# Retention and early-exit experts on one core: two tokens per partition row, 64x64 tiles of TensorE, and scatters without an order

## The chip, the core and the metric

The kernel runs on one core of one Trainium2 chip. The metric is the device time of one execution in microseconds (us). Times inside an execution come from the hardware profiler. TensorE (PE) multiplies, PEld is its loading of weights, VectorE is DVE, ScalarE is ACT, GpSimd is POOL, and SyncE (SP) issues transfers.

## What is computed

The reference has two stages. The first is a retention recurrence over 4 batches, 8 heads, 768 tokens and 64 dimensions per head, in fp32; the second lets a part of the 3072 token rows through one of 8 experts.

```python
for t in range(S):
    state = gamma * state + outer(k[t], v[t])      # per batch and head
    y[t] = scale * q[t] @ state
x = y as rows (token, 512)
do_compute = x @ w_skip > 0                        # other rows: out = x
e_idx, gate_w = top 1 of softmax(xc @ w_gate)
out[row] = x[row] + gate_w * (relu(x[row] @ w1[e_idx]) @ w2[e_idx])
```

## The kernel before

**Retention** runs in 16 units; a unit is one batch and two heads, whose two times 64 dimensions fill 128 partitions. Each unit is cut into 6 chunks of 128 tokens. `load` (L68) brings q and k of a unit so that each partition holds 6 successive tokens of a head (runs of 1536 B), and v with the token of a chunk as partition (runs of 256 B), all on SP's queue; q and k have two buffers each, v four. `scale_qk` (L173) multiplies q and k on POOL with powers of gamma, into `qks`. `t_qk` (L184) transposes them on TensorE, three 128x128 blocks into one PSUM bank with the tag T (two buffers), and ScalarE copies each bank to `QT` or `KT`, writing every sixth element, which puts the tokens back in order (L192, L193). `t_kn` (L195) transposes five chunks of `KT` back, into `Kn` with tokens as partitions. `s_at` (L206) makes the scores of a chunk for each head, 64 rows of contraction and 128 columns of keys, three chunks a call, and VectorE multiplies them with the triangular mask into `ATm` (L216). `s_kv` (L222) makes the state of each chunk from `Kn` and v (128 rows, 64 columns, 64 moving), and VectorE adds the states up into `Zb` (L230 to L238). `s_inter` (L240) adds what earlier chunks contribute and `s_av` (L253) the chunk's own values (128 rows, 64 columns, 128 moving) into one PSUM bank for each half of the chunks, `Y`; ScalarE copies it to `xT` (L263). `t_x` (L265) transposes `xT` to rows, VectorE copies them to `xall`, and SP stores a batch in six transfers.

An fp32 matmul shows as two instructions in the profile, a transpose as one.

**Gate.** Per batch, `gate_logits` (L283) and `gate_rows` (L295) find the expert, the weight and the slot of each row, and `slot_table` (L358) gathers row numbers into a table of 256 slots for each expert. They use a PSUM bank of their own, tag G.

**Experts.** The weights of the first four experts are loaded during retention by POOL's queue (fp32 in memory, bf16 on the chip); those of the last four go out after the retention stage's buffers are free (L495 to L497). `gather` (L443) fetches 128 rows of an expert by index, `x_tr` (L452) casts and transposes them, `layer1` (L462) and `layer2` (L476) multiply; for each half of 128 slots VectorE writes the new rows to `yo` (L485, four buffers), and POOL issues an indirect scatter of them to `out` (L488). `out` is one tensor, so that each scatter waits for the one before it to land.

**Order.** The loop at L379 writes out the order of one turn by hand: the transposes of unit i, the state part and the values of unit i-1, then scores, output transposes and states. From it a scheduler works out the order on each engine, allots buffers, and sets the waits; it moves work forward where the engine would be idle by its own reckoning.

Of the kernel before, what the change touches and what calls it, by code (L numbers as in the profile page):

```python
# [18 lines left out]
def kernel(  # L19
# [15 lines left out]

    nc = tc.nc
# [8 lines left out]
    R = S // 128  # L45
# [22 lines left out]
    def load(i):  # L68
        if i >= NU:
            return  # L70
        b, p = divmod(i, NP)
        hs = slice(2 * p, 2 * p + 2)
        qw[i] = pool.tile([128, 2, R * D], FP32, tag="qw", bufs=2, name="qw")
        kw[i] = pool.tile([128, 2, R * D], FP32, tag="kw", bufs=2, name="kw")
        vn[i] = pool.tile([128, 2, NCH, D], FP32, tag="vn", bufs=4, name="vn")
        nc.sync.dma_start(out=qw[i][:, :, :], in_=q[b, hs].rearrange("h (p r) d -> p h (r d)", p=128))
        nc.sync.dma_start(out=kw[i][:, :, :], in_=k[b, hs].rearrange("h (p r) d -> p h (r d)", p=128))
        for h in range(2):
# [6 lines left out]

    nrow_i = poolC.tile([128, R], I32, name="nrow_i")
    G_.iota(nrow_i[:, :], pattern=[[1, R]], base=0, channel_multiplier=R)
    nrow = poolC.tile([128, R], FP32, name="nrow")
    V_.tensor_copy(nrow[:, :], nrow_i[:, :])
    nlg = poolC.tile([128, H, R], FP32, name="nlg")  # L90
    for h in range(H):
        V_.tensor_scalar(nlg[:, h, :], nrow[:, :], lng[h], None, ALU.mult)
    tq = poolC.tile([128, H, R], FP32, name="tq")
    tk = poolC.tile([128, H, R], FP32, name="tk")
# [9 lines left out]
    maskc = poolC.tile([128, 128], FP32, name="maskc")  # L104
    make_upper_triangular(nc, maskc[:, :], val=1.0, diag=True)
# [27 lines left out]
    G_.iota(chv_i[:, :], pattern=[[1, NCHT]], base=0, channel_multiplier=0)  # L133
    row_i = poolC.tile([128, NCHT], I32, name="row_i")
    G_.iota(row_i[:, :], pattern=[[0, NCHT]], base=1, channel_multiplier=1)
# [32 lines left out]
    QT, KT, Kn, AT, ATm, KV, Y, xT, xall = {}, {}, {}, {}, {}, {}, {}, {}, {}  # L168
# [4 lines left out]
    def scale_qk(i):  # L173
        if i >= NU:
            return
        p = i % NP
        hs = slice(2 * p, 2 * p + 2)
        for w, t in ((qw, tq), (kw, tk)):
            o = pool.tile([128, R, 2, D], FP32, tag="qks", bufs=4, name="qks")
            sc = t[:, hs, :].rearrange("p h r -> p r h").unsqueeze(3).to_broadcast([128, R, 2, D])  # L180
            G_.tensor_tensor(o[:, :, :, :], w[i][:, :, :].rearrange("p h (r d) -> p r h d", d=D), sc, ALU.mult)  # L181
            w[i] = o

    def t_qk(i, w, dst, tag, bufs, a):  # L184

        if a == 0:
            dst[i] = pool.tile([128, S], FP32, tag=tag, bufs=bufs, name=tag)
        ps = ptile()
        for r in range(HB):
            in_ = w[i][:, a * HB + r, :, :].rearrange("p h d -> p (h d)")  # L190
            PE.transpose(out=ps[:, r * 128 : (r + 1) * 128], in_=in_, identity=ident[:, :])  # L191
        o = dst[i][:, :].rearrange("p (t r) -> p r t", r=R)[:, a * HB : (a + 1) * HB, :]  # L192
        A_.copy(out=o, in_=ps[:, :].rearrange("p (r t) -> p r t", r=HB))  # L193

    def t_kn(i, a):  # L195

        n = HB if a == 0 else HB - 1
        if a == 0:
            Kn[i] = pool.tile([128, NCH - 1, 128], FP32, tag="Kn", bufs=2, name="Kn")
        ps = ptile()  # L200
        for r in range(n):
            c = a * HB + r
# [37 lines left out]
    def s_inter(i, a):  # L240
        Y[i, a] = psum.tile([128, HW], FP32, tag=f"Y{a}", bufs=1, name="yps")
        first = True
        for r in range(HB):
            c = a * HB + r
            if c == 0:
                continue
# [318 lines left out]
```

## Time and profile before

| | us |
|---|---|
| median of 3 runs | 321.63 |
| lowest and highest of them | 320.69 and 322.49 |
| the profiled execution, its own time | 322.3 |
| span in it, first to last instruction | 320.4 |
| TensorE matmul busy | 240.1 (75%) |
| TensorE weight load busy | 183.8 (57%) |
| VectorE busy | 132.5 (41%) |
| ScalarE busy | 102.5 (32%) |
| GpSimd busy | 96.0 (30%) |

The mean granted clock of TensorE is 0.882 of full speed. Busy times are sums over stages with different limits; which engine bounds a stage is read from views of that stage. Neighbouring matmuls overlap in the records, so the time of a group is taken from its start to the start of the next group.

### The profile page before, as it was taken

What the parts mean: (1) busy time and instruction counts of PE and PEld (TensorE: products, weight loads), DVE (VectorE), ACT (ScalarE), POOL (GpSimd) and SP (SyncE); (2) the same over time, 40 slices, a digit from 0 to 9 for tenths busy, and PEclk for the clock granted to TensorE, in tenths of its full rate; (3) what the DMA queues carried; (4) which work ended last, traced back from release to release, by engine and by line L of the source; (5) the groups of instructions that cost most, each with busy time, mean ns of one, the idle gap of its engine ahead of it and who ended that gap; (6) DMA issues with size and microseconds to landing.
All of it is one profiled execution on the core that took longest, in us unless ns stands there. A gap on an engine that the chain in (4) does not pass through costs nothing. (4 is left out here: it accounts for less than half of the span.)

```text
span 320.4 us, 5739 instructions
## 1 busy us (share of the span) xinstructions
PE 240.1 (75%) x2253; PEld 183.8 (57%) x2253; DVE 132.5 (41%) x456; ACT 102.5 (32%) x175; POOL 96.0 (30%) x96
## 2 busy tenths in 40 slices
PE   1897999966999998999999993087995009889200
PEld 1676887746887687878787752065764004556000
DVE  4145444634666538854379436032423003223100
ACT  2462466421544454444743420021333000222000
POOL 7325550305331133213300001778500003222321
PEclk9998999995799999999999995569999557999855
DMA  8999999999994872353300023977999971111110
GB/s 215 229 198 250 248 217 213 233 209 295 336 237 102 271 213 70 91 149 101 147 3 0 2 84 114 233 250 182 175 210 209 210 141 49 42 66 54 52 74 28
DMA packets 53438, 49.67 MB, mean 155 GB/s; under 512 B 28074, under 2 KB 44458, under 8 KB 53408
## 3 DMA queue, kind: packets, MB, share of 16 engines
q0 software_dynamic: 15104, 24.07, 36.9%
q1 hardware_dynamic: 38304, 25.19, 28.3%
q8 instruction: 20, 0.33, 0.4%
q14 instruction: 10, 0.08, 0.1%
HBM read 56.64 MB, written 10.49 MB: 210 GB/s over the span
## 5 line engine op out<-in xcount | busy, mean ns | idle before, releaser
L216 DVE TENSOR_TENSOR ATm<-atps,maskc 128x384 f32<-128x384 f32 x64 | 32.7, 553 | 67.3 <-PE atps L214 67.3
L480 PE MATMUL yps<-w2b,hT 128*128 128x512 bf16 x128 | 31.3, 396 | 22.0 <-DVE yo L485 22.0
L191 PE MATMUL tps<-ident,qks 128*128 128x128 f32 x192 | 39.7, 304 | 10.7 <-POOL qks L181 6.5
L193 ACT COPY QT<-tps 128x384 f32<-128x384 f32 x32 | 26.0, 863 | 66.6 <-PE tps L191 66.6
L473 ACT ACTIVATE hT<-hps 128x512 bf16<-128x512 f32 x32 | 19.0, 597 | 82.3 <-PE hps L469 63.0
L181 POOL TENSOR_TENSOR qks<-qw,tq 128x768 f32<-128x768 f32 x16 | 23.9, 1495 | 61.1 <-PE tps L191 41.1
L214 PE MATMUL atps<-QT,KT 64*128 64x128 f32 x384 | 38.5, 298 | 0.0
L488 POOL DMA_INDIRECT out_dram<-yo,si x16 | 15.7, 980 | 71.7 <-DVE yo L485 38.9
L191 PEld LDWEIGHTS tps<-ident,qks 128*128 128x128 f32 x192 | 25.1, 156 | 20.3 <-POOL qks L181 8.0
L181 POOL TENSOR_TENSOR qks<-kw,tk 128x768 f32<-128x768 f32 x16 | 24.0, 1498 | 39.4 <-DMA kw<-in_k_dram 29.3
L214 PEld LDWEIGHTS atps<-QT,KT 64*128 64x128 f32 x384 | 32.3, 194 | 5.7 <-issue 2.8
L485 DVE SCALAR_TENSOR_TENSOR yo<-yps,g,xg 128x512 f32<-128x512 f32 x16 | 12.0, 750 | 53.8 <-DMA out_dram<-yo,si 48.7
L480 PEld LDWEIGHTS <-hT 128*128 128x128 bf16 x128 | 12.7, 101 | 36.6 <-issue 24.8
L469 PE MATMUL hps<-xgT,w1b 128*128 128x256 bf16 x256 | 31.5, 281 | 1.7 <-ACT hT L473 1.7
L247 PE MATMUL yps<-QT,Zb 128*128 128x128 f32 x160 | 30.4, 297 | 0.0
L238 DVE TENSOR_TENSOR Zb<-kvps,Zb 64x64 f32<-64x64 f32 x128 | 28.5, 222 | 4.0
L469 PEld LDWEIGHTS <-w1b 128*128 128x128 bf16 x256 | 25.8, 101 | 7.5 <-issue 2.0
L193 ACT COPY KT<-tps 128x384 f32<-128x384 f32 x32 | 25.6, 864 | 8.9 <-PE tps L191 8.8
L257 PE MATMUL yps<-ATm,vn 128*64 128x128 f32 x384 | 26.9, 280 | 0.0
L247 PEld LDWEIGHTS yps<-QT,Zb 128*128 128x128 f32 x160 | 25.7, 209 | 1.4 <-DVE Zb L236 0.7
L257 PEld LDWEIGHTS yps<-ATm,vn 128*64 128x64 f32 x384 | 21.6, 138 | 2.8 <-issue 1.3
L263 ACT COPY xT<-yps 128x384 f32<-128x384 f32 x32 | 15.3, 489 | 14.6 <-PE yps L257 14.2
(101 smaller groups left out, 248.3 us busy)
## 6 DMA issues: line engine op xcount, KB each, us to landing
w1b<-in_moe_w_dram POOLq DMA_DIRECT2D x8, 1024.0 KB
w2b<-in_moe_w_dram POOLq DMA_DIRECT2D x8, 1024.0 KB
qw<-in_q_dram SPq DMA_DIRECT2D x16, 384.0 KB, 5.4
kw<-in_k_dram SPq DMA_DIRECT2D x16, 384.0 KB, 5.1
vn<-in_v_dram SPq DMA_DIRECT2D x32, 192.0 KB, 4.8
out_dram<-xall SPq DMA_DIRECT2D x24, 256.0 KB, 3.1
xg<-out_dram,gi POOLq DMA_INDIRECT x16
out_dram<-yo,si POOLq DMA_INDIRECT x16
```

The costliest lines, as they stand in the source:

```text
L181: G_.tensor_tensor(o[:, :, :, :], w[i][:, :, :].rearrange("p h (r d) -> p r h d", d=D), sc, ALU.mult)
L191: PE.transpose(out=ps[:, r * 128 : (r + 1) * 128], in_=in_, identity=ident[:, :])
L193: A_.copy(out=o, in_=ps[:, :].rearrange("p (r t) -> p r t", r=HB))
L214: PE.matmul(out=ps[h][:, r * C : (r + 1) * C], lhsT=KT[i][hp, cs], rhs=QT[i][hp, cs], start=True, stop=True)
L216: V_.tensor_tensor(out=ATm[i][:, h, a * HB : (a + 1) * HB, :], in0=ps[h][:, :].rearrange("p (c t) -> p c t", c=HB), in1=maskc[:, :].unsque ...
L238: V_.tensor_tensor(z, kv, Zb[i % 2][c - 1][hp, hp], ALU.add)
L247: PE.matmul(out=Y[i, a][:, r * C : (r + 1) * C], lhsT=Zb[i % 2][c - 1][:, :], rhs=QT[i][:, c * C : (c + 1) * C], start=first, stop=False, ...
L257: PE.matmul(out=Y[i, a][64 * h : 64 * h + 64, r * C : (r + 1) * C], lhsT=vn[i][:, h, c, :], rhs=ATm[i][:, h, c, :], start=False, stop=True ...
L469: PE.matmul(out=ps[:, f, :], lhsT=w1b[e][:, db, fb * 128 : (fb + 1) * 128], rhs=xgT[e][:, db, :], start=(db == 0), stop=(db == NDB - 1),)
L473: A_.activation(out=hT[:, 2 * f2 : 2 * f2 + 2, :], in_=ps[:, :, :], func=AF.Relu, bias=0.0, scale=1.0)
L480: PE.matmul(out=ps[:, :], lhsT=hT[:, fb, st * 128 : (st + 1) * 128], rhs=w2b[e][:, fb, :], start=(fb == 0), stop=(fb == NFB - 1),)
L488: G_.indirect_dma_start(out=out[:, :], out_offset=bass.IndirectOffsetOnAxis(ap=si[:, st, e : e + 1], axis=0), in_=yo[:, :], in_offset=None ...
```

## The change

q, k and v are all loaded with two successive tokens in each partition row (runs of 512 B), three groups of 256 tokens a head; one transfer for v instead of two. A chunk of 128 tokens is then half of the partitions of a group, with its even and its odd tokens in two slots. Transposed blocks go to `QT` and `KT` without a stride, and the k that POOL scaled serves the states directly, so `t_kn` and `Kn` go. Scores, states and values are cut into 64x64 tiles: two heads by two chunks, each with 64 rows of contraction and 64 columns, the row halves writing to different PSUM banks. States take two banks, so the gate's bank is given up and the gate uses the two of tag T. The mask becomes 16 pieces of 64x64. The copies of `t_x` move from VectorE to ScalarE; a batch is stored in three transfers after its second half. The turn is put in another order, and output transposes and gate come one unit later. In the expert stage the scatters of the first pass are declared free of dependence on each other. Row numbers in the table, and scale factors, follow the new layout.

```diff
-    R = S // 128
+    R = 2
+    G = S // (128 * R)
...
+        for w, src, tag, bufs in ((kw, k, "kw", 2), (qw, q, "qw", 2), (vn, v, "vn", 4)):
+            w[i] = pool.tile([128, 2 * G, R * D], FP32, tag=tag, bufs=bufs, name=tag)
             nc.sync.dma_start(
-                out=vn[i][:, h, :, :], in_=v[b, 2 * p + h].rearrange("(c p) d -> p c d", p=128)
+                out=w[i][:, :, :],
+                in_=src[b, hs].rearrange("h s d -> (h s) d").rearrange("(g p r) d -> p g (r d)", p=128, r=R),
             )
...
+    maskc = poolC.tile([128, 4, R, 64], FP32, name="maskc")
+    for r in range(4):
+        for rq in range(R):
+            for hi in range(2):
+                V_.memset(maskc[64 * hi : 64 * hi + 64, r, rq, :], 1.0)
+                G_.affine_select(
+                    out=maskc[64 * hi : 64 * hi + 64, r, rq, :], in_=maskc[64 * hi : 64 * hi + 64, r, rq, :],
+                    pattern=[[R, 64]], base=rq - r % 2, channel_multiplier=-R, compare_op=ALU.is_ge, fill=0.0,
+                )
...
+        for w, t, tag in ((kw, tk, "ks"), (qw, tq, "qs")):
+            o = pool.tile([128, NCH, 2, D], FP32, tag=tag, bufs=2, name=tag)
+            sc = t[:, hs, :].rearrange("p h c -> p c h").unsqueeze(3).to_broadcast([128, NCH, 2, D])
+            in_ = w[i][:, :, :].rearrange("p (h g) (r d) -> p (g r) h d", h=2, d=D)
+            G_.tensor_tensor(o[:, :, :, :], in_, sc, ALU.mult)
...
-    def t_kn(i, a):
-
...
+        for j in range(HB):
+            in_ = w[i][:, a * HB + j, :, :].rearrange("p h d -> p (h d)")
+            PE.transpose(out=ps[:, j * 128 : (j + 1) * 128], in_=in_, identity=ident[:, :])
+        A_.copy(out=dst[i][:, a * HB : (a + 1) * HB, :], in_=ps[:, :].rearrange("p (j t) -> p j t", j=HB))
...
+        for j in range(HB):
+            s_ = a * HB + j
+            g = s_ // R
+            for c in range(2):
+                for h in range(2):
+                    hp = slice(64 * h, 64 * h + 64)
+                    cp = slice(64 * c, 64 * c + 64)
+                    PE.matmul(
+                        out=ps[h][cp, j * C : (j + 1) * C], lhsT=KT[i][hp, s_, cp], rhs=QT[i][hp, R * g : R * g + R, cp],
+                        start=True, stop=True,
+                    )
...
+                in1=maskc[:, a : a + HB, :, :].rearrange("p c r t -> p c (r t)"), op=ALU.mult,
...
+        ps = [psum.tile([128, G * D], FP32, tag=f"KV{c}", bufs=1, name="kvps") for c in range(2)]
+        for g in range(G):
+            for r in range(R):
+                for c in range(2):
+                    if 2 * g + c == NCH - 1:
+                        continue
+                    cp = slice(64 * c, 64 * c + 64)
+                    for h in range(2):
+                        PE.matmul(
+                            out=ps[c][64 * h : 64 * h + 64, g * D : (g + 1) * D], lhsT=kw[i][cp, R * g + r, h, :],
+                            rhs=vn[i][cp, h * G + g, r * D : (r + 1) * D], start=(r == 0), stop=(r == R - 1),
+                        )
...
+    def s_inter(i):
+        for c in range(2):
+            Y[i, c] = psum.tile([128, G, C], FP32, tag=f"Y{c}", bufs=1, name="yps")
+        for ch in range(1, NCH):
+            g, c = divmod(ch, 2)
...
+    def s_av(i):
+        for g in range(G):
+            for r in range(R):
+                for c in range(2):
+                    cp = slice(64 * c, 64 * c + 64)
+                    for h in range(2):
+                        PE.matmul(
+                            out=Y[i, c][64 * h : 64 * h + 64, g, :], lhsT=vn[i][cp, h * G + g, r * D : (r + 1) * D],
+                            rhs=ATm[i][cp, h, R * g + r, :], start=False, stop=(r == R - 1), skip_group_check=True,
+                        )
+        xT[i] = pool.tile([128, NCH, 128], FP32, tag="xT", bufs=6, name="xT")
+        for c in range(2):
+            A_.copy(
+                out=xT[i][:, :, 64 * c : 64 * c + 64], in_=Y[i, c][:, :, :].rearrange("p g (r t) -> p (g r) t", r=R)
+            )
...
+        for j in range(HB):
+            PE.transpose(out=ps[:, j * 128 : (j + 1) * 128], in_=xT[i][:, a * HB + j, :], identity=ident[:, :])
+        A_.copy(
+            out=xall[b][:, a * HB : (a + 1) * HB, p * 128 : (p + 1) * 128],
+            in_=ps[:, :].rearrange("p (j t) -> p j t", j=HB),
...
+        if p == NP - 1 and a == 1:
+            for g in range(G):
+                row0 = b * S + g * 128 * R
+                nc.sync.dma_start(
+                    out=out[row0 : row0 + 128 * R, :].rearrange("(p r) d -> p r d", r=R),
+                    in_=xall[b][:, R * g : R * g + R, :],
+                )
...
+            gp = ptile("gps")
...
-    for i in range(NU + 3):
+    for i in range(NU + 5):
         if i < NU:
+            scale_qk(i + 1)
             load(i + 3)
-            scale_qk(i + 1)
-            t_qk(i, qw, QT, "QT", 3, 0)
-            t_qk(i, qw, QT, "QT", 3, 1)
+            t_qk(i, kw, KT, "KT", 2, 0)
+            t_qk(i, qw, QT, "QT", 2, 0)
+            t_qk(i, kw, KT, "KT", 2, 1)
+            t_qk(i, qw, QT, "QT", 2, 1)
+        if 2 <= i < NU + 2:
+            t_x(i - 2, 0)
         if 1 <= i <= NU:
-            s_inter(i - 1, 0)
-            s_inter(i - 1, 1)
+            s_inter(i - 1)
+        if 2 <= i < NU + 2:
+            t_x(i - 2, 1)
         if i < NU:
-            t_qk(i, kw, KT, "KT", 2, 0)
-            t_qk(i, kw, KT, "KT", 2, 1)
+            s_at(i, 0)
+            s_kv(i)
         if 1 <= i <= NU:
-            s_av(i - 1, 0)
-            s_av(i - 1, 1)
+            s_av(i - 1)
         if i < NU:
-            t_kn(i, 0)
-            t_kn(i, 1)
-            s_at(i, 0)
             s_at(i, 1)
-        if 1 <= i <= NU:
-            t_x(i - 1, 0)
-            t_x(i - 1, 1)
-        if i < NU:
-            s_kv(i)
-        if i >= 1:
-            b, p = divmod(i - 1, NP)
+        if i >= 2:
+            b, p = divmod(i - 2, NP)
             if p == NP - 1 and b < B:
                 gs[b] = gate_logits(b)
             if p == 0 and b >= 1:
                 gate_rows(b - 1, gs[b - 1])
             if p == 1 and b >= 1:
-                slot_table(pool, psum, list(range((b - 1) * NCH, b * NCH)), "G")
+                slot_table(pool, psum, list(range((b - 1) * NCH, b * NCH)), "T", 2)
...
-            G_.indirect_dma_start(
+            sc = G_.indirect_dma_start(
                 out=out[:, :], out_offset=bass.IndirectOffsetOnAxis(ap=si[:, st, e : e + 1], axis=0),
                 in_=yo[:, :], in_offset=None, bounds_check=N - 1, oob_is_err=False,
             )
+            if first:
+                for o in scatters:
+                    tc.declare_no_dep(sc.ins, o.ins, reason="the slots of a pass name distinct rows")
+                scatters.append(sc)
```

## Rows read from the trace of the kernel before

**Rows 1.** Windows by stage: us, busy (instructions) per engine, PEclk, DMA share, GB/s.

```profile
0.00:78.30 78.30, 62.51 (x595) 50.59 (x596) 33.72 (x127) 31.23 (x51) 31.20 (x38) 0.93 1.10 229
78.30:188.00 109.70, 105.60 (x1158) 86.33 (x1160) 67.59 (x241) 50.17 (x88) 25.48 (x18) 0.97 0.45 131
...
244.70:263.50 18.80, 0.17 (x4) 0.05 (x1) 0.01 (x1) 0.60 (x1) 0.00 (x0) 0.59 1.04 190
263.50:298.50 35.00, 31.67 (x193) 18.73 (x192) 10.01 (x17) 7.16 (x12) 9.78 (x10) 0.93 0.13 53
```

**Rows 2.** The chain that ended last, its shares of the span by line.

```profile
by line: DMA out_dram<-yo,si 6.9%; issue 2.8%; POOL out_dram L488 0.3%; POOLq L488 0.1%; POOLq L520 0.0%
```

**Rows 3.** Waits: who waited for whom, us in total, times, longest.

```profile
DVE yo L485 <- DMA out_dram<-yo,si: 48.7, 12, 20.6
...
PE yps L480 <- DVE yo L485: 22.0, 4, 19.4
```

**Rows 4.** Timeline of POOL, VectorE and TensorE around the scatters: start, us, what.

```profile
226.13 0.98 POOL L165 DMA_DIRECT2D w2b<-in_moe_w_dram  x1
227.42 1.06 POOL L488 DMA_INDIRECT out_dram<-yo,si  x1 [0.30 <-DVE xb L456]
...
263.49 0.75 DVE L485 SCALAR_TENSOR_TENSOR yo<-yps,g,xg 128x512 f32<-128x512 f32 x1 [20.55 <-DMA out_dram<-yo,si]
264.25 1.05 POOL L488 DMA_INDIRECT out_dram<-yo,si  x1 [35.60 <-DVE yo L485]
...
294.88 3.62 PE L480 MATMUL yps<-w2b,hT 128*128 128x512 bf16 x16
...
313.74 0.97 POOL L488 DMA_INDIRECT out_dram<-yo,si  x1 [2.48 <-DMA out_dram<-yo,si]
```

**Rows 5.** Timeline of TensorE: sixth, seventh and last retention unit.

```profile
74.41 1.33 PE L226 MATMUL kvps<-vn,Kn 128*64 128x64 f32 x18 [4.91 <-DMA vn<-in_v_dram]
...
78.26 1.52 PE L191 MATMUL tps<-ident,qks 128*128 128x128 f32 x6
...
174.12 0.86 PE L191 MATMUL tps<-ident,qks 128*128 128x128 f32 x6
```

**Rows 6.** Timeline of TensorE over one plain unit, 141.37 to 150.92.

```profile
141.37 0.80 PE L226 MATMUL kvps<-vn,Kn 128*64 128x64 f32 x20
142.10 0.55 PE L191 MATMUL tps<-ident,qks 128*128 128x128 f32 x3
...
145.60 1.53 PE L257 MATMUL yps<-ATm,vn 128*64 128x128 f32 x24
147.06 0.77 PE L203 MATMUL tps<-ident,KT 128*128 128x128 f32 x5
147.75 0.94 PE L214 MATMUL atps<-QT,KT 64*128 64x128 f32 x12
148.62 0.76 PE L272 MATMUL tps<-ident,xT 128*128 128x128 f32 x5
149.33 1.40 PE L214 MATMUL atps<-QT,KT 64*128 64x128 f32 x12
150.66 0.33 PE L272 MATMUL tps<-ident,xT 128*128 128x128 f32 x1
150.92 0.80 PE L226 MATMUL kvps<-vn,Kn 128*64 128x64 f32 x20
```

**Rows 7.** ScalarE's copies, by lines: busy us, mean ns.

```profile
L193 ACT COPY KT<-tps 128x384 f32<-128x384 f32 x32 | 25.6, 864 | 8.9 <-PE tps L191 8.8
...
L263 ACT COPY xT<-yps 128x384 f32<-128x384 f32 x32 | 15.3, 489 | 14.6 <-PE yps L257 14.2
```

**Rows 8.** Timeline of TensorE: the shortest spacing of small matmuls.

```profile
173.81 0.47 PE L368 MATMUL tabps<-rhsT,oh 128*128 128x40 bf16 x12
```

**Rows 9.** Windows with q alone, then the end of k with v.

```profile
104.20:105.60 1.40, 1.40 (x26) 1.23 (x21) 0.00 (x0) 1.30 (x4) 1.39 (x1) 1.00 0.48 126
106.80:108.50 1.70, 1.70 (x18) 1.40 (x15) 1.48 (x3) 0.00 (x0) 0.00 (x0) 1.00 0.90 281
```

**Rows 10.** POOL's selection of the mask, by lines.

```profile
masks.py:66 POOL TENSOR_SCALAR_AFFINE_SELECT maskc<-maskc 128x128 f32<-128x128 f32 x1 | 0.3, 285 | 0.0
```

More of the change, by code (lines that the diff above doesn't have):

```diff
@@ L209, in s_at @@
         ps = [psum.tile([128, HW], FP32, tag=f"AT{h}", bufs=1, name="atps") for h in range(2)]
-        for r in range(HB):
-            cs = slice((a * HB + r) * C, (a * HB + r + 1) * C)
-            for h in range(2):
-                hp = slice(64 * h, 64 * h + 64)
-                PE.matmul(out=ps[h][:, r * C : (r + 1) * C], lhsT=KT[i][hp, cs], rhs=QT[i][hp, cs], start=True, stop=True)
+        for j in range(HB):
[9 more added lines that the diff above has]
+                    )
         for h in range(2):
@@ L238, in s_kv @@
                     V_.tensor_tensor(z, kv, Zb[i % 2][c - 1][hp, hp], ALU.add)
[L240 to L246, printed above, removed]
+    def s_inter(i):
[3 more added lines that the diff above has]
+            g, c = divmod(ch, 2)
             PE.matmul(
-                out=Y[i, a][:, r * C : (r + 1) * C], lhsT=Zb[i % 2][c - 1][:, :], rhs=QT[i][:, c * C : (c + 1) * C],
-                start=first, stop=False, skip_group_check=True,
-            )
-            first = False
-    def s_av(i, a):
-        for r in range(HB):
-            c = a * HB + r
-            for h in range(2):
-                PE.matmul(
-                    out=Y[i, a][64 * h : 64 * h + 64, r * C : (r + 1) * C],
-                    lhsT=vn[i][:, h, c, :], rhs=ATm[i][:, h, c, :], start=False, stop=True, skip_group_check=True,
-                )
-        if a == 0:
-            xT[i] = pool.tile([128, S], FP32, tag="xT", bufs=6, name="xT")
-        A_.copy(out=xT[i][:, a * HW : (a + 1) * HW], in_=Y[i, a][:, :])
+                out=Y[i, c][:, g, :], lhsT=Zb[i % 2][ch - 1][:, :], rhs=QT[i][:, R * g : R * g + R, 64 * c : 64 * c + 64],
+                start=(ch <= 2), stop=False, skip_group_check=True,
+            )
+    def s_av(i):
[13 more added lines that the diff above has]
+            )
     def t_x(i, a):
@@ L296, in gate_rows @@
         j0 = b * NCH
-        lp = psum.tile([128, NCH, 9], FP32, tag="G", bufs=1, name="lps")
+        lp = psum.tile([128, NCH, 9], FP32, tag="T", bufs=2, name="lps")
         for c in range(NCH):
@@ L474, in layer1, with layer2 @@
         return hT
-    def layer2(e, hT, si, g):
+    scatters = []
+    def layer2(e, hT, si, g, first=False):
         for st in range(NST):
@@ L502 @@
             x_tr(e + 1)
-        layer2(e, hT, si, g)
+        layer2(e, hT, si, g, first=True)
     NPASS = (N + CAP - 1) // CAP - 1
```

82 lines of the change are left out of this document (19 added, 63 removed).

## The prediction

> **What bounds the kernel now.** I read the stages first. Up to 78.3 us the DMA engines are saturated (share 1.10); from there to 188 us TensorE is busy 105.6 of 109.7 us at a DMA share of 0.45; from 244.7 to 263.5 us no engine computes; from 263.5 to 298.5 us TensorE is busy again, and 21.9 us follow without it [rows 1]. The chain of waits says what this last stretch is: nothing but scatters of `yo` and the time between them [rows 2]. The waits name the same queue: VectorE stood 48.7 us before a `yo` until an earlier scatter had landed, and TensorE 22.0 us for a free `yps` behind it, one wait of 19.4 us and three short ones [rows 3]. The timeline shows how: the first scatter is issued at 227.42, behind the late weight loads (the last goes out at 226.13), and VectorE writes the fifth `yo` only at 263.49, after 20.55 us of waiting for that scatter to land. From there the other fifteen follow each other, the last issued at 313.74, although the last layer-2 group ended at 294.88 + 3.62 = 298.5 [rows 4].
>
> Of the sixteen retention units, the sixth still waits 4.91 us for its v; the seventh starts its transposes at 78.26 and the last at 174.12 [rows 5]: nine units of 10.65 us on average, TensorE-bound. A plain one, from one state group to the next, takes 150.92 - 141.37 = 9.55 us [rows 6].
>
> **Scatters.** Fifteen waits of one scatter for another go. What is late next is the last `yo`. After the last layer-2 matmul come its 0.75 us on VectorE and what followed the last scatter's issue before, 320.4 - 313.74 = 6.66 us; between the two next to nothing lies, as the `yo` begun at 263.49 shows, whose scatter goes out at 264.25 [rows 4]. So 7.4 us in place of 21.9: **14.5 us less**. The three short stalls of TensorE are 22.0 - 19.4 = 2.6 us [rows 3]; I take 1.0, since some restart cost may stay. The stall of 19.4 us stays: four `yo` buffers are full, and the first scatter still lies behind the weights in its queue. POOL's own issue, about 1 us a scatter, fits: an expert has two, and its layer 2 alone takes 3.62 us [rows 4]. Together 15.5 us; bounds 13 and 18.
>
> **The three matmul groups.** Before, a unit's values take 24 instructions in 1.46 us (145.60 to 147.06), its scores 0.87 and 1.33 us (the second has a wait in it), its states 0.73 us for 20: 4.39 us [rows 6]. After, each has twice the instructions, four tiles at a time: 12 groups of four for scores, 12 for values, 10 for states. No row shows a 64x64 tile. From below: the shortest spacing of weight load with matmul is 12 in 0.47 us, less the last one's length, about 26 ns [rows 8], so 104 ns a group. From above: if every load of 64 columns queues behind the last, the states' 0.73 us / 20 = 36 ns holds for each [rows 6], 144 ns a group. A column pair of the values, the same 128 moving columns, takes 2 x 61 = 122 ns. I take 130, nearest to that: 34 x 0.13 = 4.4 us, **no gain**; bounds -0.9 and +0.5 us.
>
> **What leaves the unit.** The five transposes of K go: 0.69 us (147.06 to 147.75) [rows 6]. The section from 142.10 to 145.60 takes 3.5 us because ScalarE copies four tiles at 0.864 us each; written with stride 1 they should cost what the `xT` copy of the same shape does, 0.489 us [rows 7]. ScalarE also takes over the two copies of `t_x`: six, 2.9 us back to back. Two PSUM buffers hand them over, at a price that no row gives; I take 3.4 us, under which `s_inter` fits, with 2.9 as the lower bound and the 4.5 us of before as the upper. Before, the section and `t_x` took 3.5 + 0.71 + 0.26 = 4.5 us with gate matmuls filling a hole; these have to go somewhere, I count 0.4. So 3.8 for 4.5: -0.7. Unit: 9.55 - 0.69 - 0.7 + 0, about **8.3 us**; I take 1.25 less, bounds 0.4 and 2.2. Nine units: 11.3 us (3.6 to 20). The gate tables now share the transposes' two PSUM buffers: up to 1 us for each of three batches, inside these bounds.
>
> **The stretch before 78.3 us.** A faster unit gains nothing there while its data come at the same time. Bytes are the same; v goes from runs of 256 B to 512 B, q and k from 1536 B to 512 B. q alone moves 126 GB/s at a share of 0.48, 262 per full share; k's end with v 281 at 0.90, 312 [rows 9]: short runs cost no more time per byte, so zero. The Trainium skill (DMA: Bandwidth & Descriptors, section Specifications) asks for at least 512 B a transfer for the full rate, which would make the new v loads cheaper and the result that of the fourth rival; the rows don't bear it out.
>
> **Small edits at zero.** Sixteen mask pieces on POOL of 0.285 us at most [rows 10] are 4.6 us, hidden by the first stretch, where TensorE waits for v anyway; without that cover they would cost it. One load less per unit on SP and half as many stores are SP's alone, and only make its queue shorter. `ks` is now read by the states as well, so POOL's scaling two units ahead, and SP's load queued behind it, start some 4 us later, half a unit; a lead of more than a unit hides it, else it costs up to that. The T buffers wait for ScalarE alone now; VectorE loses two copies a unit and bounds nothing. At the end, the last unit took 188 - 174.12 = 13.9 us, 3.2 more than the mean, for its states; they are computed earlier now: 1.2 us less, bounds 0 and 3.
>
> **Sum.** 15.5 + 11.3 + 1.2 = 28.0 us. The profiled execution took 322.3 us (span 320.4 and 1.9 around it), 0.7 above the median: 294.3 against it, **294 us** beside the median of 321.63.
>
> **Rivals.** First, slower: the two column tiles of one row group take turns, so that only two of four tiles run together. Then scores and values cost 24 x 122 ns each and states 20 x 73 ns, 7.3 us for 4.4: a unit of 11.2 us. Nine units lose 14.9 us; the first six lose 9.9, less 4.9 of wait for v; minus 15.5 and 1.2 that makes +3.2, **325 us**. It decides from about 210 ns a group of four. Against it: the column pairs of before do overlap in the same rows [rows 6]. The Trainium skill (TensorE: Matmul & The Clock Gate, Part 3, section The mechanism) says a weight load overlaps running matmuls only where the row group differs; that would price the change like this rival, and pairs at 36 ns a load speak against it.
>
> Second: retention gains nothing, as waits for PSUM buffers or for `ks` take the place of the copies: 322.3 - 15.5 - 1.2, **305 us**. For it: two PSUM buffers serve transposes and gates together; against it: the copies that set the section get shorter.
>
> Third: the change does not unchain the scatters, because another tracked access to `out` keeps them in order: 294 + 15.5, **309 us**. Against it: the diff names every earlier scatter of the pass.
>
> Fourth, more: v's loads at twice the rate. Up to 78.3 us, 229 x 78.3 = 17.9 MB moved, about 9.5 of it q, k, v; a third at 270 GB/s is 11.7 us, half of it saved: **288 us**. Or the planner issues a scatter ahead of some weights, or a unit falls under 7.8 us: 281 to 287.
>
> **Chances.** Forecast 0.59 (287 to 301); slower rival 0.08; no retention gain 0.12; scatters still chained 0.05; v at twice the rate 0.06; still faster otherwise 0.10. The range 281 to 308 leaves out the slower rival, the chained scatters and a few hundredths at the ends. A measurement tells 0.5% (1.6 us) from no change: faster 0.91, same 0.03, slower 0.06, the last almost all from the first rival.
>
> **What the profile after should show.** Scatters issued right after their `yo`, and the last under 2 us after it; the wait of some 19 us before layer 2 of the fourth expert still there. Units of about 8.3 us after the DMA-bound stretch, which still ends near 78 us. Values in about 1.6 us for 48 instructions, states in 1.3 for 40. `QT` and `KT` copies near 0.49 us. The forecast is wrong if groups of four cost 200 ns or more, if the units stay at 9.5 us, or if the DMA-bound stretch moves by more than 5 us.

## The result, and the profile after

The changed kernel takes 291.24 us in the median of four runs, against 321.27 us: the ratio is 0.9063 [0.9016, 0.911]. 294 us was forecast. The profiled execution took 292.6 us with a span of 290.8, against 322.3 and 320.4. With the two kernels below that hold the weights back, two of four runs came out 1.5 to 2.8% longer than the fastest, at a lower granted clock, so the middle of the two faster runs is given, and the median of all four beside it.

Views of the changed kernel follow. The windows by stage, with the columns of [rows 1], here cut where the seventh unit starts, near the first gather, and in the expert stage's stall:

```profile
0.00:83.76 83.76, 48.45 (x930) 42.04 (x931) 33.19 (x133) 21.39 (x46) 36.25 (x53) 0.86 1.07 217
83.76:188.00 104.24, 95.15 (x1883) 78.81 (x1883) 62.20 (x256) 43.39 (x97) 25.43 (x19) 0.98 0.49 151
232.00:250.50 18.50, 0.00 (x0) 0.00 (x0) 0.26 (x1) 0.00 (x0) 0.00 (x0) 0.59 1.14 216
```

TensorE is busy 48 of the first 84 us (before 62.5 of 78.3): in the first stretch it stands idle for longer than before, with the DMA engines as full (share 1.07, before 1.10). Then it is busy 95 of 104 us. The stage without computing is still there, from 232 to 250.5 us. The waits, as [rows 3]:

```profile
DVE yo L497 <- DMA out_dram<-yo,si: 22.8, 1, 22.8
...
PE yps L492 <- DVE yo L497: 21.1, 1, 21.1
```

One wait in place of twelve, and one stall of TensorE in place of four. The timeline around the scatters, as [rows 4], with VectorE, POOL and TensorE:

```profile
250.24 0.75 DVE L497 SCALAR_TENSOR_TENSOR yo<-yps,g,xg 128x512 f32<-128x512 f32 x1 [22.80 <-DMA out_dram<-yo,si]
...
278.72 3.62 PE L492 MATMUL yps<-w2b,hT 128*128 128x512 bf16 x16
...
282.38 0.75 DVE L497 SCALAR_TENSOR_TENSOR yo<-yps,g,xg 128x512 f32<-128x512 f32 x1 [0.98 <-PE yps L492]
...
283.41 0.97 POOL L500 DMA_INDIRECT out_dram<-yo,si  x1 [0.75 <-DVE yo L497]
```

The last scatter goes out at 283.41, 0.28 us after its `yo` (282.38 + 0.75), and from the end of the last layer-2 group (278.72 + 3.62) to the end of the span 8.5 us are left, where 21.9 were. A plain unit on TensorE, as [rows 6], from scores to scores:

```profile
107.06 0.89 PE L215 MATMUL atps<-QT,KT 64*64 64x128 f32 x24
107.77 0.81 PE L236 MATMUL kvps<-vn,ks 64*64 64x64 f32 x38
108.37 0.33 PE L266 MATMUL yps<-ATm,vn 64*64 64x128 f32 x2
...
108.46 1.49 PE L266 MATMUL yps<-ATm,vn 64*64 64x128 f32 x46
109.73 0.88 PE L215 MATMUL atps<-QT,KT 64*64 64x128 f32 x24
110.53 0.55 PE L200 MATMUL tps<-ident,ks 128*128 128x128 f32 x3
...
114.30 0.89 PE L215 MATMUL atps<-QT,KT 64*64 64x128 f32 x24
```

It takes 114.30 - 107.06 = 7.24 us, where it took 9.55. The starts of the fifth unit's states, of the seventh unit and of the last, as [rows 5]:

```profile
67.70 1.44 PE L236 MATMUL kvps<-vn,ks 64*64 64x64 f32 x38 [10.86 <-DMA vn<-in_v_dram]
...
83.76 0.52 PE L200 MATMUL tps<-ident,ks 128*128 128x128 f32 x3
...
165.36 0.52 PE L200 MATMUL tps<-ident,ks 128*128 128x128 f32 x3
```

These starts and the first gather (187.29, before 199.86) split the span. The fifth unit waits 10.86 us for its v, where a sixth had waited 4.91. Each line of the table is a difference between the two profiled executions:

| stretch | before, us | after, us | difference | forecast |
|---|---|---|---|---|
| to the seventh unit | 78.3 | 83.8 | +5.5 | 0 |
| nine units, seventh to last | 95.9 | 81.6 | -14.3 | -11.3 |
| last unit to first gather | 25.7 | 21.9 | -3.8 | -1.2 |
| first gather to fifth `yo` | 63.6 | 63.0 | -0.7 | 0 |
| fifth `yo` to the end | 56.9 | 40.6 | -16.4 | -15.5 |
| sum | 320.4 | 290.8 | -29.6 | -28.0 |

The profiled execution of the changed kernel is the longest of its four, and the row to the seventh unit is the one that varies by itself: the section on the first stretch has it from three more kernels.

### The profile page after: what moved, and what is told of

The parts are those of the page before. It is cut to its first block, busy times and chain, and to the rows that moved or that the text cites. A ratio compares the mean times of both kernels' runs of the same rounds, so it can differ in the third digit from the quotient of the medians.

```text
span 290.8 us, 7709 instructions
## 1 busy us (share of the span) xinstructions
PE 208.7 (72%) x3261; PEld 163.9 (56%) x3261; DVE 120.1 (41%) x440; ACT 83.9 (29%) x175; POOL 99.7 (34%) x110
## 4 chain that ended last, share of the span: by engine, by line
PE 32%; DMA 23%; issue 13%; POOL 11%; DVE 10%; SPq 8%; ACT 1%; POOLq 0%; ACTq 0%
DMA out_dram<-yo,si 12%; SPq L77 7%; DMA vn<-in_v_dram 6%; PE tps L200 6%; PE atps L215 6%; PE yps L266 5%; PE yps L255 4%; DMA qw<-in_q_dram 4%; POOL out_dram L500 4%; POOL xg L456 4%; PE tps L283 3%; DVE Zb L248 3%; PE kvps L236 2%; PE gps L302 2%; DVE ATm L220 2%
## 5 line engine op out<-in xcount | busy, mean ns | idle before, releaser
L492 PE MATMUL yps<-w2b,hT 128*128 128x512 bf16 x128 | 31.2, 401 | 21.1 <-DVE yo L497 21.1
L190 POOL TENSOR_TENSOR qs<-qw,tq 128x768 f32<-128x768 f32 x16 | 23.9, 1496 | 58.7 <-DMA qw<-in_q_dram 28.5
L190 POOL TENSOR_TENSOR ks<-kw,tk 128x768 f32<-128x768 f32 x16 | 24.0, 1499 | 31.9 <-PE tps L200 15.9
L200 PE MATMUL tps<-ident,ks 128*128 128x128 f32 x96 | 18.3, 303 | 21.3 <-POOL ks L190 20.8
L215 PE MATMUL atps<-QT,KT 64*64 64x128 f32 x768 | 31.9, 280 | 1.8 <-DVE ATm L220 1.7
L266 PE MATMUL yps<-ATm,vn 64*64 64x128 f32 x768 | 30.4, 281 | 0.0
L215 PEld LDWEIGHTS atps<-QT,KT 64*64 64x64 f32 x768 | 24.0, 136 | 6.3 <-issue 3.2
L200 PEld LDWEIGHTS tps<-ident,ks 128*128 128x128 f32 x96 | 11.1, 150 | 25.8 <-POOL ks L190 21.0
L236 PE MATMUL kvps<-vn,ks 64*64 64x64 f32 x640 | 15.5, 231 | 13.3 <-DMA vn<-in_v_dram 13.3
L266 PEld LDWEIGHTS yps<-ATm,vn 64*64 64x64 f32 x768 | 24.3, 139 | 1.4 <-issue 1.4
L201 ACT COPY KT<-tps 128x384 f32<-128x384 f32 x32 | 15.4, 480 | 33.4 <-PE tps L200 32.9
```

The lines of the kernel that those rows point to most:

```text
L190: G_.tensor_tensor(o[:, :, :, :], in_, sc, ALU.mult)
L200: PE.transpose(out=ps[:, j * 128 : (j + 1) * 128], in_=in_, identity=ident[:, :])
L215: PE.matmul(out=ps[h][cp, j * C : (j + 1) * C], lhsT=KT[i][hp, s_, cp], rhs=QT[i][hp, R * g : R * g + R, cp], start=True, stop=True,)
L236: PE.matmul(out=ps[c][64 * h : 64 * h + 64, g * D : (g + 1) * D], lhsT=kw[i][cp, R * g + r, h, :], rhs=vn[i][cp, h * G + g, r * D : (r + 1 ...
L266: PE.matmul(out=Y[i, c][64 * h : 64 * h + 64, g, :], lhsT=vn[i][cp, h * G + g, r * D : (r + 1) * D], rhs=ATm[i][cp, h, R * g + r, :], star ...
L492: PE.matmul(out=ps[:, :], lhsT=hT[:, fb, st * 128 : (st + 1) * 128], rhs=w2b[e][:, fb, :], start=(fb == 0), stop=(fb == NFB - 1),)
```

## The experiments

### The two halves, each alone

First, in the changed kernel, the scatters tracked again:

```diff
-        layer2(e, hT, si, g, first=True)
+        layer2(e, hT, si, g)
```

> The changed kernel with one line undone: the scatters of the first pass are not declared free of each other. My theory: the freedom is worth the shorter stretch from the fifth yo to the end, 56.9 us before and 40.3 after, so 16.6 us; this kernel takes 291.2 + 16 = 307 us (304 to 310), retention unchanged (first gather near 187 us). Rival: with a quicker retention the chain costs less, because other work then sets the end: 292 to 300 us.

Then the kernel before, with nothing but the scatters of the first pass set free:

```diff
+    scatters = []
...
-            G_.indirect_dma_start(
+            sc = G_.indirect_dma_start(
...
+            if first:
+                for o in scatters:
+                    tc.declare_no_dep(sc.ins, o.ins, reason="the slots of a pass name distinct rows")
+                scatters.append(sc)
...
-        layer2(e, hT, si, g)
+        layer2(e, hT, si, g, first=True)
```

> The kernel before with only the scatters declared free. My theory: the same 16.6 us, 321.3 - 16 = 305 us (302 to 308), with the wait of some 19 us before layer 2 of the fourth expert still there. With the run of the chained scatters this tells whether the two halves of the change simply add up (both savings together about 30 us). Rival: the freedom needs the new retention, and is worth under 12 us here: above 309 us.

Measured: 306.85 us, ratio 0.9448 [0.9369, 0.9527], and 306.51 us, ratio 0.9478 [0.9392, 0.9564], against 323.23 us for the kernel before, run beside them. In the waits of the first kernel:

```profile
DVE yo L497 <- DMA out_dram<-yo,si: 47.9, 12, 20.1
```

And in those of the second:

```profile
DVE yo L487 <- DMA out_dram<-yo,si: 18.7, 1, 18.7
```

With the chain the twelve waits of before are back; without it one remains. Both expectations held: each half is worth 15 to 17 us. Singly they gain 16.4 and 16.7 us, 33.1 together; the whole change gained 30.0. So they add up within some 3 us, as they lie in different stages.

### Four tiles at a time, against pairs and single tiles

Nothing but the order of instructions inside the three groups was changed. In the first kernel scores alternate over the two row halves only and values over the two column halves only, while states issue one tile's instructions in a row:

```diff
-        for j in range(HB):
+        for c, j, h in [(c, j, h) for c in range(2) for j in range(HB) for h in range(2)]:
...
-        for g in range(G):
-            for r in range(R):
-                for c in range(2):
+        for c, h, g, r in [(c, h, g, r) for c in range(2) for h in range(2) for g in range(G) for r in range(R)]:
...
+        for c, g, r, h in [(c, g, r, h) for c in range(2) for g in range(G) for r in range(R) for h in range(2)]:
```

> As the changed kernel, but the order inside the three matmul groups is altered: scores alternate over tiles of one row only (pairs instead of quads), values over tiles of one column only (pairs), states issue the instructions of one tile in a row. Theory (the price of a quad comes from neighbours running on different tiles at once): in a plain unit the 24 score instructions go from about 0.75 us to 1.3-1.5 us, the 48 values from 1.27 to 2.4-2.7 us, the 40 states from 0.64 to 2.2-2.8 us; a plain unit goes from 7.2 to about 10 us, the whole to 305-320 us. Rival (each instruction costs its own issue, whatever tile its neighbour is on): the three groups keep 0.75, 1.27 and 0.64 us within 20% and the whole stays at 288-294 us.

In the second, scores are single, states alternate over column halves, values over row halves:

```diff
+        for c, h, j in [(c, h, j) for c in range(2) for h in range(2) for j in range(HB)]:
...
+        for c, g, r, h in [(c, g, r, h) for c in range(2) for g in range(G) for r in range(R) for h in range(2)]:
...
+        for h, g, r, c in [(h, g, r, c) for h in range(2) for g in range(G) for r in range(R) for c in range(2)]:
```

> The other choice of orders: scores issue one tile's instructions in a row, values alternate over tiles of one row, states over tiles of one column. Theory (overlap of tiles): 24 scores 2.2-2.8 us, 48 values 2.4-2.7 us, 40 states 1.2-1.4 us; the whole 305-320 us. If pairs in one row overlap and pairs in one column don't (or the other way round), the two runs show it as a factor of two between the groups. Rival (issue alone): the groups stay at 0.75, 1.27 and 0.64 us, the whole at 288-294 us.

Measured: 314.48 and 310.78 us, one run each, both in the expected range. Where the groups touch, the scheduler mixed them, so the long runs of one kind are read. The timeline of TensorE in a plain unit of the first kernel:

```profile
112.22 0.94 PE L215 MATMUL atps<-QT,KT 64*64 64x128 f32 x20
112.93 0.27 PE L236 MATMUL kvps<-vn,ks 64*64 64x64 f32 x2
...
113.16 1.55 PE L236 MATMUL kvps<-vn,ks 64*64 64x64 f32 x33
114.49 0.33 PE L266 MATMUL yps<-ATm,vn 64*64 64x128 f32 x2
...
114.76 1.87 PE L266 MATMUL yps<-ATm,vn 64*64 64x128 f32 x38
116.36 0.32 PE L215 MATMUL atps<-QT,KT 64*64 64x128 f32 x1
...
117.82 0.55 PE L200 MATMUL tps<-ident,ks 128*128 128x128 f32 x3
```

And in one of the second:

```profile
107.92 1.36 PE L215 MATMUL atps<-QT,KT 64*64 64x128 f32 x20
109.02 0.27 PE L236 MATMUL kvps<-vn,ks 64*64 64x64 f32 x1
...
109.35 0.80 PE L236 MATMUL kvps<-vn,ks 64*64 64x64 f32 x26
109.94 0.32 PE L266 MATMUL yps<-ATm,vn 64*64 64x128 f32 x1
...
110.16 2.08 PE L266 MATMUL yps<-ATm,vn 64*64 64x128 f32 x40
111.98 0.32 PE L215 MATMUL atps<-QT,KT 64*64 64x128 f32 x1
...
113.60 0.55 PE L200 MATMUL tps<-ident,ks 128*128 128x128 f32 x3
```

From each start to the next different instruction, per instruction (the granted clock is 1.00 in all three units):

| | four tiles (changed kernel) | two in the same rows | two in the same columns | one tile |
|---|---|---|---|---|
| scores | 0.71 us / 24 = 30 ns | | 0.71 / 20 = 36 | 1.10 / 20 = 55 |
| states | 0.60 / 38 = 16 | 0.59 / 26 = 23 | | 1.33 / 33 = 40 |
| values | 1.27 / 46 = 28 | 1.60 / 38 = 42 | 1.82 / 40 = 46 | |

The 136 instructions from the first scores to the next transposes take 3.47 us, 5.60 and 5.68. So the price of an instruction depends on where its neighbours run: the rival, a price of its own for each, is out, and the theory holds in direction, though a pair costs 1.2 to 1.7 times a quad rather than twice, and a single tile 1.9 to 2.5 times rather than three or four. The orders also change which PSUM banks neighbours write, but the two runs of states do not: in both, neighbours write the same bank, and two tiles cost 23 ns where one costs 40. Pairs that share their rows cost about what pairs that share their columns cost (42 and 46 ns for the values). The Trainium skill (TensorE: Matmul & The Clock Gate, Part 3, section The mechanism) says that a weight load overlaps only where the row group differs; the 42 beside 46 ns, and the 23 beside 40, speak against it here.

### The first stretch: mask, buffers, run lengths

The forecast was that nothing changes before the seventh unit. How far its start varies by itself shows in three kernels whose first stretch is that of the changed one: with the scatters tracked again (above), with the new rows in place, and with these and one small iota made early (both below). They start the seventh unit at 80.7, 82.6 and 80.7 us. TensorE in the first of them:

```profile
80.69 0.52 PE L200 MATMUL tps<-ident,ks 128*128 128x128 f32 x3
```

The kernel before starts it at 78.3 us, and at 79.1 with free scatters. So the change costs this stretch 1.6 to 5.5 us, of which the profiled execution shows the most, and a start between 80.7 and 84 us tells no kernel from the changed one.

Four kernels looked for the 5.5 us. The mask by four selections in place of sixteen:

```diff
+    V_.memset(maskc[:, :, :, :], 1.0)
+    for u in range(2):
+        for hi in range(2):
+            mv = maskc[64 * hi : 64 * hi + 64, 2 * u : 2 * u + 2, :, :]
+            G_.affine_select(
+                out=mv, in_=mv, pattern=[[-1, 2], [1, R], [R, 64]], base=0, channel_multiplier=-R,
+                compare_op=ALU.is_ge, fill=0.0,
+            )
```

> The changed kernel with the mask built by 4 selections on POOL and 1 fill on VectorE in place of 16 and 16. My step 'mask pieces at zero, hidden by the first stretch' stands against the trace: the seventh unit starts at 83.76 us, 5.5 us later than before, and POOL's first scaling at 8.56 in place of 4.97. Theory that the mask is not covered: POOL scales 3 to 4 us earlier, the seventh unit starts near 79 to 80, total 286 to 288 us. Rival, that another cause delays the first stretch (loads, two buffers for q and k): seventh unit still at 83 to 84, total 290 to 292 us.

Measured: 291.11 us, ratio 0.8983 [0.8899, 0.9067], an interval that overlaps the changed kernel's. POOL's first scaling starts at 6.01 in place of 8.56, and the seventh unit at 80.99, which lies in the spread above. So a cost of the sixteen pieces is not shown. Three buffers for q and k:

```diff
-        for w, src, tag, bufs in ((kw, k, "kw", 2), (qw, q, "qw", 2), (vn, v, "vn", 4)):
+        for w, src, tag, bufs in ((kw, k, "kw", 3), (qw, q, "qw", 3), (vn, v, "vn", 4)):
```

> The changed kernel with three instead of two buffers for the q and the k tiles. Theory (the dip of the DMA share at 30-35 us comes from the third q load waiting for one of two buffers, and the queued weight loads behind it): the third q load goes out without a wait, the dip closes, the seventh unit starts at 78-81 us instead of 83.8, and the whole falls to 286-288.5 us. Rival (the first stretch is bound by the DMA engines or by POOL's order, and a sooner q only delays the weights): the seventh unit starts within 1.5 us of 83.8 and the whole stays at 289.5-293 us.

Measured: 292.35 us, ratio 0.9099 [0.9051, 0.9148]; the seventh unit at 83.9. What the extra buffers were to cure is this dip. In a window of the changed kernel:

```profile
32.00:34.00 2.00, 0.00 (x0) 0.00 (x0) 0.00 (x0) 0.00 (x0) 1.98 (x3) 0.50 0.07 18
```

The same window with three buffers:

```profile
32.00:34.00 2.00, 0.00 (x0) 0.00 (x0) 1.29 (x4) 0.00 (x0) 0.00 (x0) 1.00 1.18 320
```

The dip goes, and 9.39 MB of q, k and v have moved by 78 us in place of 8.07. But the seventh unit starts no earlier: the theory falls, and the rival stands. Then the length of runs. q and k in runs of 1536 B, everything else as changed:

```diff
+            if tag == "vn":
...
+            else:
+                nc.sync.dma_start(
+                    out=w[i][:, :, :].rearrange("p (h g) x -> p h (g x)", h=2),
+                    in_=src[b, hs].rearrange("h (p r) d -> p h (r d)", p=128),
+                )
```

> The changed kernel with q and k read in runs of 1536 B again (six successive tokens to a partition), everything else as it is: the tokens of q and k then stand in another order, so it computes another recurrence, and the experts get other rows; only the stretch before the seventh unit is read. Theory (runs of 512 B in place of 1536 B cost the hardware queue more engine time per byte, and that is part of why the seventh unit starts at 83.8 and not at 78.3): the queue of q, k, v moves 5% or more bytes per unit of its time than in the changed kernel, and the seventh unit starts at 78-81 us. Rival (the run length costs nothing; the order in which weight loads and q, k, v share the engines sets the start): the bytes per unit of time stay within 3%, and the seventh unit starts at 82.5 us or later.

And v alone in runs of 256 B:

```diff
+            if tag == "vn":
+                nc.sync.dma_start(
+                    out=w[i][:, :, :].rearrange("p a (r d) -> p (a r) d", r=R),
+                    in_=src[b, hs].rearrange("h s d -> (h s) d").rearrange("(x p) d -> p x d", p=128),
+                )
+            else:
...
```

> The changed kernel with v read in runs of 256 B, as before the change (q and k stay at 512 B); the tokens of v then stand in another order, so it computes something else, and only the stretch before the seventh unit is read. Theory (the shorter the runs, the more time of the DMA queue a byte costs): over the first 78 us the queue of q, k, v moves 10% or more fewer bytes per unit of its share than the 8.07 MB at 43.5% of the changed kernel (0.186 MB per per cent), so 0.168 or less, and the seventh unit starts at 85 us or later. Rival (256 B and 512 B runs cost the same per byte, only q and k matter): 0.18 to 0.19, and the seventh unit within 1.5 us of 83.8.

The queue of q, k and v over the first 78 us (packets, MB, share of the 16 engines), in the kernel before:

```profile
q1 hardware_dynamic: 16613, 9.41, 47.8%
```

In the changed kernel:

```profile
q1 hardware_dynamic: 17103, 8.07, 43.5%
```

With q and k in 1536 B:

```profile
q1 hardware_dynamic: 12676, 11.34, 49.6%
```

With v in 256 B:

```profile
q1 hardware_dynamic: 22606, 8.52, 49.4%
```

| runs of q, k / of v | MB per per cent of share | seventh unit at |
|---|---|---|
| 1536 / 256 B (before) | 9.41 / 47.8 = 0.197 | 78.3 |
| 512 / 512 B (after) | 8.07 / 43.5 = 0.186 | 83.8 |
| 1536 / 512 B | 11.34 / 49.6 = 0.229 | 66.0 |
| 512 / 256 B | 8.52 / 49.4 = 0.172 | 84.0 |

These rates repeat: five other kernels with runs of 512 B have 0.183 to 0.188, and the kernel before with free scatters has 0.198. The starts of the seventh unit with long q and k, and with short v:

```profile
65.99 0.52 PE L206 MATMUL tps<-ident,ks 128*128 128x128 f32 x3
```

```profile
84.01 0.52 PE L206 MATMUL tps<-ident,ks 128*128 128x128 f32 x3
```

The queue's bytes go the way of the theory both times. Shorter runs move 7% fewer in a share of time, where 10% was expected. Longer runs move 23% more; but with them up to 1.6 MB of finished rows, stored by the same queue, are among these bytes. Over the first 70 us, before any row is stored, the queue's rows with long q and k and of the changed kernel are:

```profile
q1 hardware_dynamic: 10775, 9.01, 45.6%
```

```profile
q1 hardware_dynamic: 14860, 6.95, 42.0%
```

That is 0.198 against 0.165 MB per per cent of 70 us, 19% more.

The start follows only one way. Longer q and k bring the seventh unit 15 to 18 us forward, further than the expected 78 to 81; shorter v leaves it at the late end of the spread, near where the rival has it, so that a shift under some 3 us could not be seen. The price of a byte is shown, then; how much of it turns into a later start is not, and that the order in which weight loads and q, k, v come to the engines counts too was not tried by itself.

### The weights out of the first stretch

POOL issues the eight early weight loads of 1 MB by 48 us. Here each waits for the scaled k of a later unit, one load for every second unit:

```diff
-            load_w(*wjobs.pop(0), poolW)
+            load_w(*wjobs.pop(0), poolW, after=kw[min(i + 1, NU - 1)])
...
+            if after is not None:
+                G_.tensor_copy(w1b[e][:, 0, 0:1], after[:, 0, 0, 0:1])
```

> The changed kernel itself, only with the eight early weight loads held back, one for every second unit (no in-place rows). Theory (what was left of the gain in retention sat in the first stretch, which the weight loads and q, k, v share): retention ends about 22-28 us earlier as it did in the in-place version, the expert stage is as it was, and the whole falls from 291.2 to 264-272 us. Rival (the expert stage's stall on the queue of scatters gives part of it back): the first gather comes as early, but the stretch from the first gather to the end grows by 4 us or more, and the whole stays above 272 us.

Measured: 266.2 us (268.19 in the median of four runs); the profiled execution took 266.45, against 292.6. Windows of it, columns as above:

```profile
0.00:40.00 40.00, 29.74 (x605) 25.64 (x605) 23.80 (x105) 15.22 (x33) 25.84 (x45) 1.00 1.00 221
40.00:80.00 40.00, 36.71 (x760) 30.60 (x762) 22.15 (x84) 16.81 (x38) 15.47 (x13) 1.00 1.09 272
```

Its timeline of TensorE, the seventh unit:

```profile
56.14 0.52 PE L204 MATMUL tps<-ident,ks 128*128 128x128 f32 x3
```

TensorE is busy 66 of the first 80 us; the seventh unit starts at 56.1 in place of 83.8, and the first gather goes out at 161.5 in place of 187.3: 25.8 of the 26.2 us gained. From there to the end it takes 103.1 us, where it took 103.5, so nothing is given back. The theory holds. What held the first stretch back was that 8.4 MB of weights go through the DMA engines together with q, k and v, long before they are needed. Their company raises the price of a byte, too: over the first 50 us the queue of q, k, v moves 9.38 MB at a share of 72.2% here and 5.84 MB at 47.9% in the changed kernel, 7% more per share at the same run lengths.

### The stall of the expert stage

One wait for a `yo` buffer stayed. If the new rows overwrite the gathered ones, there is none to wait for:

```diff
-            yo = poolE.tile([128, DM], FP32, tag="yo", bufs=4, name="yo")
+            yo = xg[e, st]
```

> The changed kernel with the new rows written over xg in place of four yo buffers, so that no write waits for a scatter. My theory: the 21.1 us that TensorE waits for the fifth yo come from four buffers behind a scatter that lies in the queue after the late weights; without them TensorE goes on at 230 us, the last weights land near 250 us and are not needed before, so layer 2 of the last expert ends near 261 and the total is 270 to 273 us. Rival: TensorE then waits for the weights of the late experts instead, and the end stays within 6 us: 285 to 291 us.

Measured: 284.37 us, ratio 0.8758 [0.8682, 0.8834], a miss by more than 10 us. Its waits say why:

```profile
DVE thr L526 <- POOL thr_i L524: 19.5, 1, 19.5
...
PE hps L479 <- DVE xgT L470: 13.7, 1, 13.7
```

VectorE now waits for `thr_i`, a small iota for the test after the first pass. In this kernel it stands on POOL behind the eighth scatter, and the copies of `xgT` stand behind that wait on VectorE. So the iota and its copy were moved to the start of the kernel:

```diff
+    thr_i = poolC.tile([128, NPASS], I32, name="thr_i")
+    G_.iota(thr_i[:, :], pattern=[[CAP, NPASS]], base=CAP, channel_multiplier=0)
+    thr = poolC.tile([128, NPASS], FP32, name="thr")
+    V_.tensor_copy(thr[:, :], thr_i[:, :])
...
-    thr_i = poolE.tile([128, NPASS], I32, tag="thr_i", bufs=1, name="thr_i")
...
```

> The in-place version (new rows written over the gathered ones, no buffers of their own) with the iota of thr_i and its copy moved to the start of the kernel, so that VectorE no longer waits in the expert stage for an instruction that stands on POOL behind the scatters. Theory (that false wait of 19.5 us was what took back the gain of the in-place version): TensorE's wait near 253 us falls under 3 us and the whole comes to 268-275 us. Rival (late weights of the last expert bound the stage, whatever VectorE waits for): TensorE still waits 8 us or more before the fourth expert and the whole stays at 280-285 us.

Measured: 267.92 us, ratio 0.8319 [0.8282, 0.8356]. After the first transposes of the stage the trace shows no wait of TensorE longer than 0.3 us. The theory holds. With the weights held back as well, by the edit above:

> The in-place version with the row thresholds made early, and in it the eight weight loads of the first four experts held back, one for every second unit: each waits for a one-column copy on POOL that reads the scaled k of the next unit. Theory (the first stretch is slow because 8 MB of weights share the DMA engines with q, k, v there, while the DMA share is about 0.5 later): the first seven units go at 8-9.5 us each, the seventh starts at 65-72 us instead of about 83, the later units slow from 9.0 to at most 9.5 us, and the whole falls from 267.9 to 252-260 us. Rival (what the weights take later costs as much as what is gained early, or the copies delay POOL): the first gather comes no more than 3 us earlier, and the whole stays at 265-272 us.

Measured: 243.4 us (246.45 in the median of four runs), below the expected 252 to 260; the seventh unit starts at 55.3, also earlier than the expected 65 to 72. Windows of its profiled execution (241.89 us), columns as above:

```profile
0.00:60.00 60.00, 48.71 (x1014) 42.01 (x1016) 32.55 (x135) 24.62 (x53) 34.36 (x53) 1.00 1.03 239
60.00:130.00 70.00, 67.24 (x1362) 55.70 (x1352) 44.12 (x166) 30.70 (x69) 27.64 (x25) 1.00 0.95 236
```

TensorE is granted its full clock (1.00, 2.4 GHz) through 130 us; in the changed kernel the first stretch had 0.86, with 0.50 (1.2 GHz) in the row of the dip, after TensorE had stood idle.

This version beats the kernel before and the changed one. The two edits add up: 23.3 us for the rows in place, 24.5 more for the weights, which alone gave 25.1.

## Why the prediction was right, and where it was not

**The total** was right, 294 for 291.24 us, and for the reasons named: freed scatters and shorter units. But its 28.0 us are met by errors that cancel: +5.5 us where nothing was forecast, and some 7 us more gain elsewhere. That they cancel so nearly is luck.

**Scatters.** Right: 15.5 forecast, 16.4 measured behind the fifth `yo`, 0.7 before it, and 15 to 17 us in both single-half kernels. The tail shrank by 21.9 - 8.5 = 13.4 (forecast 14.5); the rest is that layer 2 no longer stops, 35.0 us from the fifth `yo` to the last group before, 32.1 after. The stall that was to stay did, at 21.1 us.

**The three matmul groups.** The mechanism was right, the size off: 34 quads were put at 130 ns, 4.4 us and no gain. Measured are 3.47 us, 102 ns a quad. The term that fails is the states': 16 ns an instruction, 64 ns a quad, under the lower bound of 26 ns and 104. That bound came from matmuls of 40 columns on the whole array [rows 8], which says nothing of neighbours on different tiles. The first rival (tiles of one row group take turns) made a quad cost 244 ns for scores and values and 146 for states; measured are 118, 110 and 64, far from its 210, so it does not happen here.

**What leaves the unit.** The section with transposes took 110.53 to 114.30, 3.77 us, forecast 3.8. The copies are right, too; those of `KT` and `xall`, by lines, busy us and mean ns, as [rows 7]:

```profile
L201 ACT COPY KT<-tps 128x384 f32<-128x384 f32 x32 | 15.4, 480 | 33.4 <-PE tps L200 32.9
L284 ACT COPY xall<-tps 128x384 f32<-128x384 f32 x32 | 15.2, 479 | 9.8 <-PE tps L283 8.8
```

So the unit's 7.24 us for 8.3 is the groups' 0.9 us and little else. Of the 2.3 us that a plain unit lost, the mean over nine units shows 14.3 / 9 = 1.6: a mean unit lay 10.65 - 9.55 = 1.1 us above a plain one, now 9.07 - 7.24 = 1.8. The gate thus costs more, some 2 us for each of three batches, where up to 1 us was allowed. Waits explain little of it: in these nine units the profile has TensorE waiting 1.9 us in all, 1.7 of them for `ATm`, where it had waited 3.2 before. What the rest is, no run tells apart.

**The end of retention.** 3.8 us for 1.2, beyond the upper bound of 3. That its states are computed earlier was the reason given; no run tried it alone.

**The first stretch.** Wrong: the profiled execution lost 5.5 us, beyond the prediction's own mark of 5, and the three kernels with the same first stretch 2.4 to 4.3. The step that failed is "short runs cost no more time per byte, so zero". It took rates from two windows of 1.4 and 1.7 us in which the engines were not full [rows 9], and one of them mixed k with v. The queue's rows over the full stretch say otherwise: 0.197 MB per per cent before, 0.186 after, 0.229 with long runs of q and k. The Trainium skill (DMA: Bandwidth & Descriptors, section Specifications) asks for at least 512 B; v does gain from 256 to 512 B (0.172 to 0.186), as that rule has it and the prediction denied. But from 512 to 1536 B q and k gain as well, which that rule would not let one expect. How the loss divides between dearer bytes and the changed order of loads stays open, for starts and rates did not go together in every kernel. The later scaling of `ks`, which was let cost up to 4 us, is not the cause: in this stretch POOL waits 36.4 us for q and k to land and 9.0 us for transposes, and never for the states. The sixteen mask pieces were put at zero, and no run shows that they cost more.

**The rivals.** Retention gained (second), the scatters were freed (third); v's cheaper runs (fourth) brought no earlier start: 84.0 us with 256 B, 80.7 to 83.8 with 512.

## What to carry to other kernels

Price a change of layout by its run lengths for every tensor that it touches, and read that price from a stretch in which the queue is saturated. Where transfers that are needed late share a saturated stretch with those needed now, hold them back: that was worth some 25 us here, nearly as much as the whole change. And a wait that vanishes exposes the next one in line, here a three-line test queued behind it, so look at what stands behind a stalled instruction on each engine.

## What had not been expected of the hardware

Instructions of 64 moving columns on four 64x64 tiles follow each other at 16 ns, those on one tile at 40. Run length counts above 512 B too: over the first 70 us, 0.165 MB per per cent of the engines with 512 B for q and k, against 0.198 with 1536. And indirect scatters on POOL's queue went out only as earlier weight transfers landed, though they share no data with them; whether the queue holds them or a wait that the scheduler set, no run shows. Timeline of POOL in the changed kernel, after the first scatter (214.77):

```profile
220.31 1.03 POOL L500 DMA_INDIRECT out_dram<-yo,si  x1 [4.49 <-DMA w2b<-in_moe_w_dram]
225.22 0.97 POOL L500 DMA_INDIRECT out_dram<-yo,si  x1 [3.88 <-DMA w1b<-in_moe_w_dram]
230.28 0.97 POOL L500 DMA_INDIRECT out_dram<-yo,si  x1 [4.08 <-DMA w2b<-in_moe_w_dram]
231.26 0.16 POOL L524 IOTA thr_i<- 128x11 int32 x1
```

Three scatters stand 3.9 to 4.5 us each until weights have landed, by the profile's reckoning. The row after them is the iota that became the next wait in the in-place version.
